# Pooling attention into a maxout feed-forward: the attention output of batches 3 to 7 turned by the DMA crossbar instead of TensorE

## The chip, the cores and the metric

The kernel runs on one core of a Trainium2 chip. The metric is the device time of one execution in microseconds, the median of several runs. The profile is one execution taken by the hardware profiler; its span is a little shorter than the timed run.

A core has five engines that work at the same time and meet at semaphores: TensorE (PE; PEld is its weight load), VectorE (DVE), ScalarE (ACT), GpSimd (POOL) and SyncE (SP), which here only issues DMAs. Each engine takes its instructions in the order of the program.

## The reference

Attention with pooled keys and values, for 8 batches of 8 heads, 576 queries, 64 elements a head. Then a feed-forward layer over all 4608 tokens, with three weights whose results are joined by a maximum.

```python
k_p = k.reshape(B, H, 72, 8, D).mean(axis=3)       # 576 keys pooled to 72
v_p = v.reshape(B, H, 72, 8, D).mean(axis=3)
attn = softmax(q @ k_p^T / sqrt(D)) @ v_p          # B, H, S, D
x = attn.transpose(0, 2, 1, 3).reshape(4608, 512)
h = maximum(x @ w1, x @ w2, x @ w3)                # 512 -> 768
out = h @ w_out                                    # 768 -> 512, float32
```

## The kernel before

The feed-forward layer is the larger part. It runs in nine blocks of 512 tokens (the loop over `n`), each in 22 slots. `hidden(n)` has 18 slots: for each of six column blocks of 128 and each of the three weights, four matmuls of 128x512 (L272) into a PSUM tile of the group "pw", and then ACT (L277) and DVE (L280, L283) take the maximum into `hT`. `project(n)` has 4 slots of six matmuls (L305); ACT copies the result (L310) and SP stores it in two DMAs of 128 KB (L314). `hidden` reads `xT`, the attention output with the channels on the partitions, for all 4608 tokens.

The attention of batch b is cut into steps, which are laid between the slots. `PLAN` gives, for each step in turn, the slot of iteration n after which it is issued, for batch n+1; `PLAN1` does so for n=1. Steps that the plan leaves over run in the first eight slots of the next iteration (`side`). The steps of a batch are:

- `queries(b)`: four `turn_q` steps (TensorE transposes of q, L159, copied by ACT at L161), one `turn_k` (the pooled keys transposed, copied by DVE at L171), and eight `scores` steps, one per head (matmuls L194, exponential on ACT L199).
- `outputs(b)`: five chunks of 128 tokens, `v0` to `v4` and `x0` to `x4`. `values` (step v) multiplies by the pooled values (L223), and DVE divides by the sum (L229, L231) into the tile `xn`, tokens on the partitions. `turn_x` (step x) transposes it: four 128x128 transposes on TensorE (L214) into the PSUM tile `pxt`, and a copy by ACT (L218) into `xT`. The last chunk starts at token 448 and keeps its upper 64 tokens.

`turn_q`, `turn_k` and `turn_x` share one PSUM buffer, the tag "tr". Batches 576 tokens long and blocks of 512 tokens shift against each other: block 3 needs batch 3 up to its token 320, block 4 batch 4 up to 256, block 5 batch 5 up to 192, block 6 batch 6 up to 128, block 7 batch 7 up to 64.

k and v of batches 2 to 7 are pooled on POOL by folding (`fold`, L127 and L130). POOL also issues the loads of k, v and q from batch 3 on (`load_k` L71, `load_v` L77, `load_q` L86), into two buffers each. In iteration n POOL folds k of batch n+2, issues the load of k of batch n+3, folds v, and issues the loads of v and q. The POOL DMAs run in one queue (q0 on the page), those from SP in another (q1).

Of the kernel before, what the change touches and what calls it, by code (L numbers as in the profile page):

```python
# [14 lines left out]
def kernel(  # L15
# [11 lines left out]
    nc = tc.nc  # L27
    dt = mybir.dt
    F32, BF16, F16 = dt.float32, dt.bfloat16, dt.float16

    B, H, S, D = q.shape
# [22 lines left out]
    sb3 = ctx.enter_context(tc.tile_pool(name="sb3", bufs=3))  # L54
# [3 lines left out]
    kts, vts, qbs, kps, qTs, ets = {}, {}, {}, {}, {}, {}  # L58
# [7 lines left out]
    def load_k(b, eng, dtype=F32, parts=1):  # L66
        kts[b] = ld.tile([96, 6, POOL, D], dtype, name="kt", tag="kt")
        src = k[b].rearrange("h s d -> (h s d)").rearrange(
            "(p i j d) -> p i j d", p=96, i=6, j=POOL)
        n = 6 // parts  # L70
        return [eng.dma_start(out=kts[b][:, i:i + n], in_=src[:, i:i + n])  # L71
                for i in range(0, 6, n)][-1]

    def load_v(b, eng, dtype=F32, cuts=(0, H)):
        vts[b] = ld.tile([Sp, H, POOL, D], dtype, name="vt", tag="vt")
        src = v[b].rearrange("h (sp j) d -> sp h j d", j=POOL)
        return [eng.dma_start(out=vts[b][:, h:g], in_=src[:, h:g])  # L77
                for h, g in zip(cuts, cuts[1:])][-1]

# [17 lines left out]

    load_q(0)
    load_k(0, nc.sync, parts=3)
    warm = const.tile([128, 512], BF16, name="warm", tag="warm")  # L100
    nc.vector.memset(warm, 1.0)
    ident = const.tile([128, 128], BF16, name="ident", tag="ident")
    make_identity(nc, ident)
    identh = const.tile([128, 128], F16, name="identh", tag="identh")
    make_identity(nc, identh)
    load_v(0, nc.gpsimd, F16, (0, 4, 6, 8))
    for i in range(3):
        load_w(slice(256 * i, 256 * i + 256))
    load_k(1, nc.gpsimd, F16)
    load_q(1)  # L110
    early = load_v(1, nc.gpsimd, F16)
    nc.gpsimd.dma_start(
        out=wo_sb, in_=moe_w_out.rearrange("(jc p) c -> p jc c", p=128))
    after((load_k(2, nc.sync), load_v(2, nc.sync)), early)
    load_q(2)

# [6 lines left out]
    xT = const.tile([128, KCH, TOK], F16, name="xT", tag="xT")  # L123
# [85 lines left out]
        exp(ets[b][:, h, :], psc[0:Sp, 0:S])  # L209

    def turn_x(b, c0, keep, xn, tag, evac=nc.scalar.copy):
        pxt = psp.tile([128, KCH, 128], F16, name="pxt", tag=tag[0], bufs=tag[1])
        for kc in range(KCH):
            nc.tensor.transpose(  # L214
                pxt[:, kc, :],
                xn[:, kc // 2, 2 * (kc % 2):2 * (kc % 2) + 2, :], identh)
        g0 = S * b + c0
        evac(out=xT[:, :, g0 + keep:g0 + 128], in_=pxt[:, :, keep:128])  # L218

    def values(b, c0):  # L220
        pav = psp.tile([128, 2, 512], F32, name="pav", tag="att", bufs=2)
        for h in range(H):
            nc.tensor.matmul(  # L223
                pav[:, h // 4, 65 * (h % 4):65 * (h % 4) + 65],
                ets[b][:, h, c0:c0 + 128], vp_all[:, b, h, :],
                start=True, stop=True)
        pv = pav[:, :, 0:260].rearrange("p g (h e) -> p g h e", e=65)
        rcp = sb3.tile([128, 2, 4], F32, name="rcp", tag="rcp")
        nc.vector.reciprocal(out=rcp, in_=pv[:, :, :, 64])  # L229
        xn = sb3.tile([128, 2, 4, D], F16, name="xn", tag="xn")  # L230
        nc.vector.tensor_tensor(  # L231
            out=xn, in0=pv[:, :, :, 0:D],
            in1=rcp.to_broadcast([128, 2, 4, D]), op=ALU.mult)
        return xn
# [5 lines left out]
    def queries(b):  # L240

        new_et(b)
        for m, (n0, n1) in enumerate(((0, 5), (5, 10), (10, 14), (14, 18))):
            turn_q(b, n0, n1, nc.scalar.copy, TR)
            yield
            if m == (3 if b == 2 else 2):
                turn_k(b)
                yield
        for h in range(H):
            scores(b, h)  # L250
            yield

    def outputs(b, order="v0 v1 x0 v2 x1 v3 x2 v4 x3 x4", tag=TR, evac=nc.scalar.copy):


        xns = {}
        for step in order.split():
            i = int(step[1])
            c0, keep = CHUNKS[i]
            if step[0] == "v":  # L260
                xns[i] = values(b, c0)
            else:
                turn_x(b, c0, keep, xns[i], tag, evac)
            yield
# [121 lines left out]
    pool_v(0, 6, 8, PW, nc.vector.tensor_copy)  # L386
    scores2(0)
    xn0 = [values(0, c0) for c0, _ in CHUNKS[:2]]
    heat(1)
    turn_x(0, 0, 0, xn0[0], PW)  # L390
    scores2(2)
    heat(1)
    turn_x(0, 128, 0, xn0[1], PW, nc.vector.tensor_copy)
    scores2(4)
    heat(1)
# [25 lines left out]
    for slot, _ in enumerate(hidden(0, hT0)):  # L421
# [4 lines left out]
        if slot > 24:  # L426
            h = 4 * (slot - 25)
# [14 lines left out]

    def batch(b):
        yield from queries(b)
        yield from outputs(b, *(("v0 v1 x0 v2 x1 x2 v3 x3 v4 x4",) if b == 2 else ()))


    PLAN = (2, 4, 5, 6, 8, 8, 9, 10, 11, 12, 13, 14, 15, 16, 17, 18, 18, 19, 19, 20,
            20, 21)
    PLAN1 = (9, 11, 13, 15, 19, 20, 21, 22, 23, 24, 25, 26, 26, 27, 28, 28, 29, 29, 30,  # L450
             30)
    for n in range(1, TOK // NB):
        if n + 2 < B:
            fold_k(n + 2, nc.gpsimd)
            if n + 3 < B:
                load_k(n + 3, nc.gpsimd)
            fold_v(n + 2)
            if n + 3 < B:
                load_v(n + 3, nc.gpsimd)
                load_q(n + 3)  # L460
        hT = new_hT()
        nxt = batch(n + 1) if n + 1 < B else iter(())
        plan = PLAN1 if n == 1 else PLAN
        slot = 0
        for part in (hidden(n, hT), project(n, hT)):
            for _ in part:
                if slot < 8:
                    next(side, None)
                for _ in range(plan.count(slot)):
                    next(nxt, None)  # L470
                slot += 1
        side = nxt
# [30 lines left out]
```

The softmax here doesn't subtract the row's maximum and nothing guards it: scores larger than these inputs give would overflow.

## Time and profile before

| what | value |
|---|---|
| time, median of 3 runs | 264.18 us (264.04 to 264.33) |
| span of the profile | 262.3 us, granted TensorE clock 0.995 |
| busy: PE, DVE, ACT, POOL | 95%, 51%, 48%, 45% |
| one iteration, n=2 to 5 (from first L305 to first L305) | 26.8 us |
| of it TensorE busy | 26.75 us |
| POOL's last fold ends | 161.5 us |

The page's busy shares are averages over the span. The chain that ended last is followed back from the last instruction, at each step to what released it; time on it is time that the end depends on. An iteration's times are best read there or in the timeline of one engine.

### The profile page before, as it was taken

What the parts mean: (1) busy time and instruction counts of PE and PEld (TensorE: products, weight loads), DVE (VectorE), ACT (ScalarE), POOL (GpSimd) and SP (SyncE); (2) the same over time, 40 slices, a digit from 0 to 9 for tenths busy, and PEclk for the clock granted to TensorE, in tenths of its full rate; (3) what the DMA queues carried; (4) which work ended last, traced back from release to release, by engine and by line L of the source; (5) the groups of instructions that cost most, each with busy time, mean ns of one, the idle gap of its engine ahead of it and who ended that gap; (6) DMA issues with size and microseconds to landing.
All of it is one profiled execution on the core that took longest, in us unless ns stands there. A gap on an engine that the chain in (4) does not pass through costs nothing.

```text
span 262.3 us, 4747 instructions
## 1 busy us (share of the span) xinstructions
PE 250.3 (95%) x1902; PEld 142.6 (54%) x1902; DVE 132.7 (51%) x243; ACT 125.9 (48%) x225; POOL 117.6 (45%) x84
## 2 busy tenths in 40 slices
PE   7899999988997999999999999999999999999992
PEld 3678556675554555555555555555555554444441
DVE  4567561766344546364635463556446554523430
ACT  1464237243754574548464746464656463132221
POOL 8653000999899999899790896000000000000000
PEclk9999999999999999999999999999999999999998
DMA  7999999886698975987987705100510042015006
GB/s 185 202 197 209 199 234 226 257 202 113 157 238 180 196 182 115 231 266 139 215 239 180 113 4 132 28 2 0 121 42 0 2 110 50 4 41 119 0 12 152
DMA packets 21027, 34.73 MB, mean 132 GB/s; under 512 B 2668, under 2 KB 13548, under 8 KB 20428
## 3 DMA queue, kind: packets, MB, share of 16 engines
q0 software_dynamic: 14048, 21.44, 42.0%
q1 hardware_dynamic: 6796, 12.85, 19.3%
q8 instruction: 15, 0.25, 0.4%
q10 hardware_dynamic: 160, 0.13, 0.2%
q14 instruction: 8, 0.07, 0.1%
HBM read 34.60 MB, written 9.44 MB: 168 GB/s over the span
## 4 chain that ended last, share of the span: by engine, by line
PE 87%; DVE 4%; ACT 4%; issue 1%; DMA 1%; SPq 0%; DVEq 0%
PE pw L272 49%; PE po L305 16%; PE psc L194 6%; PE pav L223 4%; PE pqt L159 3%; PE pxt L214 3%; PE wm L326 2%; ACT xT L218 2%; PE pvp L148 1%; DVE t L280 1%; DMA out_dram<-osb 1%; ACT et L199 1%; DVE xn L231 1%; PE pkt L166 1%; DVE kz L171 1%
## 5 line engine op out<-in xcount | busy, mean ns | idle before, releaser
L272 PE MATMUL pw<-xT,mw 128*128 128x512 f16 (+1 forms) x720 | 158.1, 358 | 0.9 <-ACT xT L218 0.7
L272 PEld LDWEIGHTS <-mw 128*128 128x128 f16 x720 | 64.3, 98 | 48.5 <-issue 0.8
L280 DVE TENSOR_TENSOR t<-t,pw 128x512 f16<-128x512 f16 (+1 forms) x60 | 38.0, 633 | 75.2 <-PE pw L272 46.3
L277 ACT CAST t<-pw 128x512 f16<-128x512 f32 (+1 forms) x60 | 32.6, 543 | 41.6 <-PE pw L272 39.0
L305 PE MATMUL po<-mwo,hT 128*128 128x512 f16 (+1 forms) x222 | 51.5, 373 | 0.0
L199 ACT ACTIVATE et<-psc 72x576 f16<-72x576 f32 (+2 forms) x62 | 40.4, 661 | 16.1 <-PE psc L194 16.1
L283 DVE TENSOR_TENSOR hT<-t,pw 128x512 f16<-128x512 f16 (+1 forms) x60 | 37.9, 632 | 11.0 <-PE pw L272 7.8
L127 POOL TENSOR_TENSOR vt<-vt 72x2048 f32<-72x2048 f32 (+1 forms) x12 | 41.2, 3432 | 4.5 <-DMA vt<-in_v_dram 4.0
L127 POOL TENSOR_TENSOR kt<-kt 96x1536 f32<-96x1536 f32 (+1 forms) x12 | 31.5, 2622 | 23.2 <-DMA kt<-in_k_dram 22.6
L310 ACT COPY osb<-po 128x512 f32<-128x512 f32 (+1 forms) x36 | 20.8, 579 | 38.7 <-PE po L305 38.5
L305 PEld LDWEIGHTS <-hT 128*128 128x128 f16 x222 | 19.9, 97 | 19.4 <-DVE hT L283 1.7
L231 DVE TENSOR_TENSOR xn<-pav,rcp 128x512 f16<-128x512 f32 x40 | 27.6, 691 | 1.4
L194 PE MATMUL psc<-qT,kz 128*128 128x64 bf16 (+3 forms) x192 | 25.6, 246 | 1.2 <-DVE kz L171 1.2
L161 ACT COPY qT<-pqt 128x512 bf16<-128x512 bf16 (+1 forms) x25 | 15.9, 637 | 21.5 <-PE pqt L159 21.5
L194 PEld LDWEIGHTS <-kz 128*128 128x128 bf16 x192 | 17.5, 98 | 15.0 <-DVE kz L171 2.0
L218 ACT COPY xT<-pxt 128x512 f16<-128x512 f16 (+1 forms) x34 | 18.6, 547 | 4.3 <-PE pxt L214 4.2
L223 PEld LDWEIGHTS <-et 72*128 72x128 f16 x320 | 15.2, 98 | 4.6 <-issue 0.5
L223 PE MATMUL pav<-vp,et 72*128 72x65 f16 x320 | 17.2, 194 | 0.4 <-ACT et L199 0.4
L214 PEld LDWEIGHTS <-xn 128*128 128x128 f16 x160 | 11.7, 97 | 10.7 <-DVE xn L231 3.1
L229 DVE RECIPROCAL rcp<-pav 128x8 f32<-128x8 f32 x40 | 8.2, 204 | 18.4 <-PE pav L223 18.3
L214 PE MATMUL pxt<-identh,xn 128*128 128x128 f16 x160 | 15.5, 219 | 2.0 <-DVE xT L218 0.7
L159 PEld LDWEIGHTS <-qb 128*128 128x128 bf16 x144 | 10.0, 97 | 7.9 <-issue 2.4
(43 smaller groups left out, 116.8 us busy)
## 6 DMA issues: line engine op xcount, KB each, us to landing
out_dram<-osb SPq DMA_DIRECT2D x70, 128.0 KB, 2.4
kt<-in_k_dram POOLq DMA_DIRECT2D x5, 1152.0 KB, 8.3
vt<-in_v_dram POOLq DMA_DIRECT2D x5, 1152.0 KB, 10.0
qb<-in_q_dram POOLq DMA_DIRECT2D x7, 576.0 KB, 13.3
mw<-in_moe_w_dram POOLq DMA_DIRECT2D x9, 256.0 KB, 10.0
kt<-in_k_dram SPq DMA_DIRECT2D x3, 384.0 KB, 4.8
kt<-in_k_dram SPq DMA_DIRECT2D x1, 1152.0 KB, 10.0
vt<-in_v_dram SPq DMA_DIRECT2D x1, 1152.0 KB
```

Of the source, the lines that this page charges most:

```text
L127: e.tensor_tensor(out=t[:, :, 0:n, :], in0=t[:, :, 0:n, :], in1=t[:, :, n:2 * n, :], op=ALU.add)
L194: nc.tensor.matmul(out, kz_all[b % 2][:, f % 2, h, :], qTs[b][:, n + i0:n + i1, 64 * (h % 2):64 * (h % 2) + 64], start=True, stop=True)
L199: nc.scalar.activation(out=out, in_=in_, func=FT.Exp, scale=1.0 / 64.0)
L214: nc.tensor.transpose(pxt[:, kc, :], xn[:, kc // 2, 2 * (kc % 2):2 * (kc % 2) + 2, :], identh)
L218: evac(out=xT[:, :, g0 + keep:g0 + 128], in_=pxt[:, :, keep:128])
L223: nc.tensor.matmul(pav[:, h // 4, 65 * (h % 4):65 * (h % 4) + 65], ets[b][:, h, c0:c0 + 128], vp_all[:, b, h, :], start=True, stop=True)
L231: nc.vector.tensor_tensor(out=xn, in0=pv[:, :, :, 0:D], in1=rcp.to_broadcast([128, 2, 4, D]), op=ALU.mult)
L272: nc.tensor.matmul(pw, w_sb[wi][:, kc, bass.ts(jc, 128)], xT[:, kc, col], start=(kc == 0), stop=(kc == KCH - 1))
L277: nc.scalar.copy(out=t, in_=pw)
L280: nc.vector.tensor_tensor(out=t1, in0=t, in1=pw, op=ALU.max)
L283: nc.vector.tensor_tensor(out=hT[:, jc, c0:c1], in0=t, in1=pw, op=ALU.max)
L305: nc.tensor.matmul(po, hT[:, jc, bass.ts(mm, 128)], wo_sb[:, jc, c], start=(jc == 0), stop=(jc == JCH - 1))
```

## The change

The chunks of batches 3 to 7 no longer go through TensorE, PSUM and ACT. SP issues a transposing DMA that reads `xn` in SBUF and writes `xT` in SBUF. This is to free TensorE of the transposes. The tile `xn` gets six buffers instead of three. The steps of each batch but batch 2 run in the order v0 x0 v1 x1 and so on, and the plan has one more entry, so that all steps of a batch are done within the iteration: the query transposes start at slot 0 instead of 2, and x0 follows v0 in slot 16.

The loads of k and v from batch 3 on are cut into pieces of 1 KB: a k load into runs of 256 elements (it had runs of all of a partition's 12 KB), a v load into two DMAs, one for each half of the eight rows that are pooled (runs of 2 KB before). The smaller pieces are to let other transfers in between.

```diff
 def load_k
-        return [eng.dma_start(out=kts[b][:, i:i + n], in_=src[:, i:i + n])
+        return [eng.dma_start(out=kts[b][:, i:i + n], in_=src[:, i:i + n],
+                              max_dma_last_dim=256 if b > 2 else None)
                 for i in range(0, 6, n)][-1]
 def load_v
         src = v[b].rearrange("h (sp j) d -> sp h j d", j=POOL)
+        if b > 2:
+            for j in (0, 4):
+                eng.dma_start(out=vts[b][:, :, j:j + 4], in_=src[:, :, j:j + 4])
+            return
 def turn_x
+        if b > 2:
+            g0 = S * b + c0
+            nc.sync.dma_start_transpose(
+                out=xT[:, :, g0 + keep:g0 + 128],
+                in_=xn.rearrange("p g h d -> p (g h d)")[keep:128])
+            return
 def values
-        xn = sb3.tile([128, 2, 4, D], F16, name="xn", tag="xn")
+        xn = sb3.tile([128, 2, 4, D], F16, name="xn", tag="xn", bufs=6)
 def batch
-        yield from outputs(b, *(("v0 v1 x0 v2 x1 x2 v3 x3 v4 x4",) if b == 2 else ()))
+        yield from outputs(b, "v0 v1 x0 v2 x1 x2 v3 x3 v4 x4" if b == 2
+                           else "v0 x0 v1 x1 v2 x2 v3 x3 v4 x4")
-    PLAN = (2, 4, 5, 6, 8, 8, 9, 10, 11, 12, 13, 14, 15, 16, 17, 18, 18, 19, 19, 20,
-            20, 21)
+    PLAN = (0, 2, 4, 5, 7, 8, 9, 10, 11, 12, 13, 14, 15, 16, 16, 17, 17, 18, 18, 19,
+            19, 20, 20)
```

## The prediction

> **What bounds the kernel now.** I read the page first: busy shares, the slices, the chain that ended last, the groups. Each row of the groups gives busy time, then the mean of one.
>
> ```profile
> PE 250.3 (95%) x1902; PEld 142.6 (54%) x1902; DVE 132.7 (51%) x243; ACT 125.9 (48%) x225; POOL 117.6 (45%) x84
> ...
> DMA  7999999886698975987987705100510042015006
> ...
> PE 87%; DVE 4%; ACT 4%; issue 1%; DMA 1%; SPq 0%; DVEq 0%
> ...
> L218 ACT COPY xT<-pxt 128x512 f16<-128x512 f16 (+1 forms) x34 | 18.6, 547 | 4.3 <-PE pxt L214 4.2
> ...
> L214 PE MATMUL pxt<-identh,xn 128*128 128x128 f16 x160 | 15.5, 219 | 2.0 <-DVE xT L218 0.7
> ```
>
> TensorE is the bound. ACT and DVE stand at half, and the DMA engines are near full only until about slice 22 (145 us). So a cut in TensorE's own instructions counts in full; ACT's copies count only where TensorE waits for them. The 219 ns of a transpose is a latency in the pipeline and not its price. The price is in the chain in order of time (start, length, what), here at the end of iteration n=3 and the start of n=4:
>
> ```profile
> 160.02 0.22 PE pxt L214 x4
> 160.25 0.26 PE pav L223 x8
> 160.51 1.31 PE po L305 x6
> 161.82 0.02 issue
> 161.84 0.25 ACT osb L310
> 162.09 0.23 issue
> 162.32 0.60 ACT xT L218
> 162.92 0.04 issue
> ```
>
> Four transposes of one chunk take 0.22 us, 55 ns each. The chain leaves TensorE at 161.82: in slot 0 of the next iteration the last chunk (x4) needs the one "tr" PSUM buffer, which ACT is still emptying from x3. Four L272 matmuls start at 161.86 and need 0.86 us, to 162.72; the transposes start at 162.96. TensorE loses 0.24 us.
>
> The third view is the timeline of one engine, for POOL (loads) and for the stores.
>
> ```profile
> 99.11 0.86 POOL L77 DMA_DIRECT2D vt<-in_v_dram  x1
> 99.96 0.78 POOL L86 DMA_DIRECT2D qb<-in_q_dram  x1
> ...
> 108.06 0.56 POOL L71 DMA_DIRECT2D kt<-in_k_dram  x1
> ```
>
> And the instructions of the tile osb in 103 to 110 us (end of n=2), then the store line L314 in 156 to 190 us (no loads left):
>
> ```profile
> L314 SPq DMA_DIRECT2D out_dram<-osb x8: 466/574/1353, 103.5 to 109.6; - x8
> DMA to landing us min/median/max: 7.0/7.4/10.6
> ...
> L314 SPq DMA_DIRECT2D out_dram<-osb x15: 466/467/827, 157.1 to 189.3; - x15
> DMA to landing us min/median/max: 2.2/2.3/4.1
> ```
>
> The same 128 KB store from SP lands in 2.3 us on quiet DMA engines, and in 7.4 us when a v load and a q load are in flight. The new transposes go down the same queue, move the same 128 KB, and TensorE will wait for some of them. This pair of numbers is the heart of the forecast.
>
> **What the Trainium skill says.** (1) "VectorE: DVE Perf Modes", The three transpose paths: a 128x128 bf16 transpose is 390 ns on TensorE and 1309 ns through the DMA crossbar. The trace has 55 ns of TensorE time in a stream, so the TensorE figure isn't what is saved here. No run yet shows a crossbar transpose. (2) "DMA: Bandwidth & Descriptors", Anatomy of one DMA: a fixed cost near 2 us for most DMAs; the quiet 2.3 us of the trace agrees. (3) Same page, Queues, rings and completion order: each DMA engine goes round the queues at packet granularity. The 7.4 us agrees with long waits for a turn. It is what smaller pieces of k and v can shorten.
>
> **The change part by part.** Let T be the start of the first L305 group of an iteration. Batches 3 to 7 are made in n=2 to 6.
>
> Removed from TensorE: 25 chunks x 4 = 100 transposes x 55 ns = 5.5 us, all on the path. Removed waits: 0.24 us at slot 0 of n=3 to 7, 1.2 us. Removed from ACT: 25 copies of xT; they were hidden behind TensorE apart from these waits, so nothing more. Sum: -6.7 us.
>
> Plan: values keep slots 16 to 20 and scores 8 to 15; query transposes move to slots 0, 2, 4, 7 and the keys from 6 to 5. In n=2 slots 0 to 2 still hold x3, v4, x4 of batch 2, on TensorE. So x3 and the first query transposes now meet in slot 0 on the one "tr" buffer. In the trace x3's transposes end at 81.02, ACT copies it from 81.31 to 81.90: +0.9 us. Slot 2 already had such a meeting (0.46 us wait at 84.44), so it adds nothing. In n=3 to 6 no transposes of xn are left there.
>
> Loads: v becomes two DMAs, k goes from 96 long runs to 1152 pieces. A POOL issue is 0.57 us for k and 0.86 us for v (576 runs); the difference over 480 runs is 0.6 ns a run. So k costs about +0.65 and v +0.87: 1.5 us of POOL a batch. It is hidden: the keys of batch 3 are folded at 71.1 and used in n=2 about slot 5, near 85; its values at 80.9, used near 100; batch 7's values at 161.5, used after 200. A batch takes POOL 18.3 us against TensorE's 26.8, so the margin grows. Slower DMA from smaller pieces is bounded likewise: 14 us of margin is over half of a batch's POOL time. Cost taken: 0. The extra xn buffers only keep DVE from waiting for the transposes to read.
>
> The new wait. Every transpose is a DMA on SP behind stores. SP's issue cost isn't in the trace for a transpose: below by a store, 0.47 us; above by the Trainium skill's column for earlier generations ("DMA: Bandwidth & Descriptors", under Why a DMA increments its semaphore): 631 cycles, and 32 cycles a tile. With tiles of 16x128 as its constraints table implies, 32 tiles give 1655 cycles, 1.4 us at SyncE's 1.2 GHz ("Trainium Kernel Development and Optimization", NeuronCore Architecture), an estimate. I take 1.0. Landing L from the start of issue: at least a quiet store plus a little, 2.5 us; at most 7.4 us as in the crowded window. I take the middle, 4.95, where loads are in flight, since smaller pieces should shorten the wait for a turn, but the q loads keep their size; where none are, 2.5.
>
> Which chunk does the next iteration need? hidden(n+1) starts at T + 4x1.30 + 3x0.26 = T+6.0 and reads tokens up to 512(n+2): in n=2 chunks 0 to 2 of batch 3, in n=3 and 4 chunks 0 and 1, in n=5 and 6 chunk 0. From the timeline of DVE in n=4 (T=181.99) xn of chunk 0 is ready at T+0.2, chunk 1 at T+1.6, chunk 2 at T+2.7 (its values come 0.2 sooner than now).
> - n=2: SP issues x1 from T+1.6 to 2.6, then the two stores of the first project step (0.47 to 0.6 us each) to T+3.7, then x2. It lands at T+3.7+4.95 = T+8.65: TensorE waits 2.7 us.
> - n=3: x1 lands at T+1.6+4.95 = T+6.6: 0.6 us.
> - n=4: the loads are nearly over, L=2.5: free. n=5, 6: T+0.2+L, free even at 5.8.
> Behind a waiting SP stand only later stores; five osb buffers cover them. TensorE in order holds everything behind the first L272, hence full price.
>
> Sum: 264.2 - 6.7 + 0.9 + 2.7 + 0.6 = 261.7 us.
>
> **Rivals.**
> Hidden transposes: L=2.5 throughout. Then n=2 waits 0.2 us, the others nothing: 264.2 - 6.7 + 0.9 + 0.2 = 258.6 us. For it: 128 KB is little beside 200 GB/s, and the pieces are cut for this. Against: the 7.0 us minimum in the very window where x0 to x2 are issued.
> Starved transposes, slower than before: L=7.4 where loads are crowded, n=2 to 4, POOL being later than now by some 1.5 us a batch. Waits T+3.7+7.4-6.0 = 5.1, then twice 1.6+7.4-6.0 = 3.0: 264.2 - 5.8 + 11.1 = 269.5 us. For it: the store rows. Against: in n=3 now stores land in 3.4 us (median).
> Serial crossbar, slower: four blocks of 1309 ns one after another, 5.2 us a chunk, SP or the crossbar the bound. n=2: 0.2+5.2x2+1.0+5.2 = T+16.8, waits 10.8; n=3 and 4: T+10.6, 4.6 each; n=5 and 6 T+5.4, free: 264.2 - 5.8 + 20 = 278.4 us. Against: the 1309 ns is likely to hold mostly fixed cost.
>
> **How the numbers follow.** Forecast case 0.45, hidden 0.22, starved 0.18, serial 0.07; 0.08 lies between forecast and starved, where the waits return all of the gain. Predicted is 261.7. The range goes from just under the hidden case, 258.0, to just over the starved one, 270.0; the serial case and half of the odd ones stay outside. Faster by over 0.2% (under 263.65): 0.67; within: 0.07; slower: 0.26.
>
> **What would show it.** TensorE should have 100 fewer L214 matmuls and ACT 25 fewer xT copies; an iteration from n=5 on should be 26.82 - 1.1 - 0.24 = 25.5 us from one first L305 to the next. The first L272 of n=3 should wait for a DMA into xT, 1 to 5 us, that of n=4 under 2 us, later ones not. SP's transposes should take 0.5 to 1.4 us to issue, and land in 4 to 6 us near 105 us and in 2.5 us after 160. POOL should finish the last fold 5 to 10 us later with nobody waiting. The forecast is wrong if transposes land slower than 6 us on quiet engines, if a transpose stops the stores or loads beside it, or if TensorE waits in n=5 or 6.

## The result, and the profile after

The changed kernel takes 276.15 us (274.14 to 276.67, four runs) against 264.25 us: ratio 1.043, 95% interval 1.038 to 1.049. It is slower by 4.3%.

The page of the changed kernel: busy shares, the granted clock in 40 slices, the packets, the chain by engine, and the first group (L283 is now the line of the first feed-forward matmul).

```profile
PE 246.6 (90%) x1801; PEld 137.5 (50%) x1802; DVE 132.1 (48%) x243; ACT 115.1 (42%) x200; POOL 128.0 (47%) x89
...
PEclk9999999999999999757999999999999999999998
...
DMA packets 34385, 37.66 MB, mean 137 GB/s; under 512 B 15068, under 2 KB 25948, under 8 KB 34268
...
q1 hardware_dynamic: 19116, 15.80, 27.1%
...
PE 75%; DMA 11%; DVE 8%; ACT 2%; issue 2%; POOL 1%; POOLq 0%; DVEq 0%
...
L283 PE MATMUL pw<-xT,mw 128*128 128x512 f16 (+1 forms) x720 | 159.6, 360 | 15.5 <-DMA xT<-xn 14.6
```

TensorE has some 100 instructions fewer, ACT 25, and both are less busy. The DMA engines, 1% of the chain before, are 11% of it. The 14.6 us at the end of the last row are waits of `hidden` for a transpose, two of them. The chain in order of time shows the large one, at the end of n=2 (start, length, what):

```profile
106.41 1.30 PE po L316 x6
107.71 0.28 PE pav L234 x8
108.17 14.41 DMA xT<-xn
122.62 1.89 PE pw L283 x4
124.51 0.53 PE pqt L164 x5
125.04 2.52 PE pw L283 x8
```

x2 of batch 3 was issued at 108.17 and landed 14.4 us later. TensorE had finished its last L316 matmul at 109.3 and stood still for 13.4 us. Then a second loss begins: four matmuls take 1.89 us instead of 0.86. The table of stretches (length, then busy time of PE, PEld, DVE, ACT, POOL, then clock, DMA share, GB/s) shows why:

```profile
122.60:124.60 2.00, 1.98 (x7) 0.88 (x8) 0.00 (x0) 0.06 (x1) 1.36 (x2) 0.50 1.44 198
124.60:126.60 2.00, 2.00 (x10) 0.91 (x8) 0.00 (x0) 1.17 (x2) 0.00 (x0) 0.52 1.13 153
126.60:128.60 2.00, 2.00 (x15) 1.06 (x14) 1.38 (x2) 0.69 (x1) 0.00 (x0) 1.00 1.43 225
```

The clock granted after the wait is half for 3.9 us. (It had fallen to half within the wait, near 112.8, some 3.5 us after TensorE stopped.) From 122.62 to 127.56 the chain has 4 matmuls in 1.89 us, 5 in 0.53 and 8 in 2.52, where a full clock takes 0.86, 0.28 and 1.73: 2.1 us lost.

The difference of the spans is 274.9 - 262.3 = 12.6 us. The parts: -5.5 (100 transposes) -1.2 (waits in slot 0) +0.9 (the meeting of x3 and the first query transposes) +1.2 (a new wait, below) +13.4 and +1.2 (x2 at n=2, x1 at n=3) +2.1 (clock) = +12.1. The rest of 0.5 us is not assigned.

The tile xT answers how the transposes behave: first those issued at 103 to 105 us (x0 and x1 of batch 3), then those of 197 us and later, when no load is left.

```profile
L219 SPq DMA_TRANSPOSE xT<-xn x2: 1313/1578/1842, 103.5 to 105.0; - x2
DMA to landing us min/median/max: 12.1/12.7/13.2
...
L219 SPq DMA_TRANSPOSE xT<-xn x10: 1188/1232/1422, 197.6 to 233.3; - x10
DMA to landing us min/median/max: 2.4/2.5/4.0
```

A transpose costs SP 1.2 us and lands in 2.5 us on quiet DMA engines, about as a store of the same 128 KB. Beside v5, q5 and k6 (the loads of batches 5 and 6) the same instruction takes 12 to 14 us to land, and the issue of x2 alone keeps SP for 4.2 us. How the two kinds meet can be read from the DMA queues in one stretch, 119 to 121.2 us (packets, MB, share):

```profile
q0 software_dynamic: 86, 0.35, 47.4%
q1 hardware_dynamic: 94, 0.04, 37.3%
```

In this stretch q0 (the loads) and q1 (transposes and stores) send about the same number of packets, but q0 moves nine times the bytes. It does not hold for the whole wait: from the issue of x2 to its landing q0 sends 808 packets with 1.61 MB, q1 1842 with 0.87 MB. Over the whole kernel q1 has 12,320 packets and 2.95 MB more than before (19,116 and 15.80 MB against 6796 and 12.85 MB). The 25 transposes move 20 x 131 KB + 5 x 66 KB = 2.95 MB, so their packets average 240 bytes: a chunk of 128 KB is over 500 packets, some 32 on each of 16 DMA engines. The Trainium skill says that the rounds between the queues go by packets ("DMA: Bandwidth & Descriptors", Queues, rings and completion order). The stretch of 119 to 121.2 us agrees with it, and this stream has very small packets.

### The profile page after: what moved, and what is told of

Its sections match the earlier page's. It is cut to its first block, busy times and chain, and to the rows that moved or that the text cites. A ratio compares the mean times of both kernels' runs of the same rounds, so it can differ in the third digit from the quotient of the medians.

```text
span 274.9 us, 4608 instructions
## 1 busy us (share of the span) xinstructions
PE 246.6 (90%) x1801; PEld 137.5 (50%) x1802; DVE 132.1 (48%) x243; ACT 115.1 (42%) x200; POOL 128.0 (47%) x89
## 3 DMA queue, kind: packets, MB, share of 16 engines
q1 hardware_dynamic: 19116, 15.80, 27.1%
## 4 chain that ended last, share of the span: by engine, by line
PE 75%; DMA 11%; DVE 8%; ACT 2%; issue 2%; POOL 1%; POOLq 0%; DVEq 0%
PE pw L283 45%; PE po L316 15%; DMA xT<-xn 8%; PE psc L199 5%; PE pqt L164 3%; DVE kz L176 3%; DMA vt<-in_v_dram 3%; PE pav L234 3%; DVE hT L294 1%; PE pvp L153 1%; DVE t L291 1%; PE pxt L225 1%; DVE xn L242 1%; ACT xT L229 1%; ACT et L204 1%
## 5 line engine op out<-in xcount | busy, mean ns | idle before, releaser
L283 PE MATMUL pw<-xT,mw 128*128 128x512 f16 (+1 forms) x720 | 159.6, 360 | 15.5 <-DMA xT<-xn 14.6
L283 PEld LDWEIGHTS <-mw 128*128 128x128 f16 x720 | 64.7, 98 | 66.0 <-DMA xT<-xn 15.6
L316 PE MATMUL po<-mwo,hT 128*128 128x512 f16 (+1 forms) x222 | 51.5, 373 | 0.0
L294 DVE TENSOR_TENSOR hT<-t,pw 128x512 f16<-128x512 f16 (+1 forms) x60 | 38.0, 633 | 13.3 <-PE pw L283 10.7
L316 PEld LDWEIGHTS <-hT 128*128 128x128 f16 x222 | 19.9, 97 | 19.4 <-DVE hT L294 1.7
L234 PEld LDWEIGHTS <-et 72*128 72x128 f16 x320 | 15.9, 98 | 7.5 <-issue 0.5
L91 POOL DMA_DIRECT2D qb<-in_q_dram x9 | 7.0, 783 | 19.3 <-PE pqt L164 16.9
L164 PE MATMUL pqt<-ident,qb 128*128 128x128 bf16 x144 | 13.3, 222 | 2.7 <-ACT xT L229 1.4
L135 POOL TENSOR_TENSOR kp<-kt 96x384 bf16<-96x384 f32 x12 | 11.7, 991 | 0.5
```

Source lines behind the costliest of these rows:

```text
L164: nc.tensor.transpose(pqt[:, n - n0, :], qf[:, 128 * n:128 * n + 128], ident)
L234: nc.tensor.matmul(pav[:, h // 4, 65 * (h % 4):65 * (h % 4) + 65], ets[b][:, h, c0:c0 + 128], vp_all[:, b, h, :], start=True, stop=True)
L283: nc.tensor.matmul(pw, w_sb[wi][:, kc, bass.ts(jc, 128)], xT[:, kc, col], start=(kc == 0), stop=(kc == KCH - 1))
L294: nc.vector.tensor_tensor(out=hT[:, jc, c0:c1], in0=t, in1=pw, op=ALU.max)
L316: nc.tensor.matmul(po, hT[:, jc, bass.ts(mm, 128)], wo_sb[:, jc, c], start=(jc == 0), stop=(jc == JCH - 1))
```

## The experiments

Theories: P, the transposes wait for the packets of the loads in flight. F, they are slow by themselves, in one queue behind stores or in the crossbar. S, the 1 KB pieces do the harm.

**1. The pieces alone.** The kernel before with the edits of `load_k` and `load_v` only.

> The kernel before with the loads of k and v of batches 3 to 7 in pieces of 1 KB and nothing else. Theory P (a transposed chunk is 512 small packets, 32 on each DMA engine, and each waits for a turn behind a packet of the loads; the pieces are no part of the loss): 264 us, within 0.3% of before, POOL some 7 us more busy, its last fold later with nobody waiting. Rival S (the small pieces themselves clog the DMA engines): slower than before by 2 us or more, stores in 103 to 112 us landing later than 7.4 us.

Measured: 264.14 us against 264.02, ratio 1.0006 (0.9994 to 1.0018). POOL is busy 128.2 us instead of 117.6, and nobody waits for it. The eight stores of 103.7 to 109.5 us land in 8.8 to 9.6 us (7.0 to 10.6 before), with no effect on the time. The pieces alone are free; S falls as a cause. On POOL's queue a piece is not a packet: in the packet records of the traces a v load is 288 packets of 4096 bytes with the pieces and without them, and a k load goes from 96 packets of 12,288 bytes to 288 of 4096.

This run also has the loads and the stores of the changed kernel without its transposes. What the DMA engines carry over 104 to 122 us, here and then in the changed kernel:

```profile
DMA packets 1889, 4.02 MB, mean 223 GB/s; under 512 B 288, under 2 KB 800, under 8 KB 1888
...
DMA packets 2904, 3.09 MB, mean 172 GB/s; under 512 B 1800, under 2 KB 2312, under 8 KB 2903
```

The stores issued from 106 to 108 us, here (L319) and then in the changed kernel (L325):

```profile
L319 SPq DMA_DIRECT2D out_dram<-osb x3: 467/606/731, 106.0 to 107.8; - x3
DMA to landing us min/median/max: 9.0/9.3/9.5
...
L325 SPq DMA_DIRECT2D out_dram<-osb x2: 546/566/586, 106.9 to 107.5; - x2
DMA to landing us min/median/max: 14.2/14.4/14.7
```

The load k6, issued at 112.3 us in both, lands in 9.8 us here and in 15.5 us beside the transposes. So transposes and loads together move less than stores and loads do, though packets are in flight on the engines for more of the time (a DMA share of 1.17 against 0.90 over 104 to 122 us), and the stores and the loads come late as well. The prediction had named this as a sign of being wrong. Why the engines move less was not tried.

**2. The transposes with whole loads.**

```diff
 def load_k
-                              max_dma_last_dim=256 if b > 2 else None)
+        return [eng.dma_start(out=kts[b][:, i:i + n], in_=src[:, i:i + n])
...
 def load_v
-        if b > 2:
-            for j in (0, 4):
-                eng.dma_start(out=vts[b][:, :, j:j + 4], in_=src[:, :, j:j + 4])
-            return
```

> The changed kernel with the loads of k and v as before (runs of 12 KB and 2 KB). Theory P: the v load runs as packets of 4096 bytes either way, so the wait of the first matmul of n=3 for x2 stays at 10 to 15 us; the 12 KB packets of k make a turn longer where a k load is in flight; 276 to 282 us. Rival S: the wait falls below 6 us and the time below 268 us.

Measured: 285.58 us, with runs from 274 to 290, so no ratio is given. The chain of the profiled run (287.49 us), at the same place:

```profile
106.19 1.10 PE po L311 x6
107.29 26.76 DMA xT<-xn
```

In this run x2 took 26.8 us instead of 14.4. But the fastest of the four took 274.17 us, less than the changed kernel's 276.15, so it is not shown that the pieces shorten the wait. Shown is that the loss stays without them: no run is near the 268 us of rival S. The theory's 10 to 15 us was wrong for the profiled run: v6, issued at 117.25, came into the same stretch, and over 112 to 120 us the engines moved only some 100 GB/s.

**3. Loads of v and q held until x2 has landed.** In n=2 to 4, `turned` holds the transposes of `turn_x`.

```diff
-            if n + 3 < B:
+            if n == 1:
                 load_v(n + 3, nc.gpsimd)
                 load_q(n + 3)
...
+        if n > 1 and n + 3 < B:
+            after(load_v(n + 3, nc.gpsimd) + load_q(n + 3), turned[n + 1, 256])
```

> The changed kernel with the loads of v and q of batches 5, 6 and 7 held back until x2 of the same iteration has landed, so that no load is in flight beside the transposes that TensorE waits for. Theory P: each of x0 to x2 lands within 2.3 to 3 us of its issue, the wait of 13.4 us at the start of n=3 falls below 0.5 us, TensorE keeps its full clock there, and the time is 259 to 261 us, faster than the kernel before. Rival F (the transposes are slow by themselves, one after another behind the stores on the queue of SP): x2 still lands after 8 us or more and the time stays above 270 us.

Measured: 261.25 us, ratio 0.989 (0.986 to 0.992). The profiled run is the longest of the five (263.93 us; the others took 260.56 to 261.63). With the same queue, the same stores ahead and the same crossbar, x2 lands in 3.7 us:

```profile
106.60 1.10 PE po L316 x6
107.71 3.71 DMA xT<-xn
```

TensorE waits 2.0 us instead of 13.4, not under 0.5 as expected: SP issues x2 4.2 us after the first L316 group, and it needs 3.7 us where 1.8 were left. So the time also ends a little above the 259 to 261 us expected. Half clock follows this wait too (0.50 from 112.7 to 116.0 us); the four other runs have a mean granted clock of 0.999 or 1.00, so there it can hardly have fallen. F falls as the main cause; what is left of it is those 2 us.

**4. Batch 3 on TensorE, batches 4 to 7 through the crossbar.** The order of batch 3's steps and the plan of n=2 are those of the kernel before.

```diff
-        if b > 2:
+        if b > 3:
```

> The changed kernel with batch 3 left on TensorE (its order and the plan of n=2 as before); batches 4 to 7 go through the crossbar. Its x4 runs in slot 0 of n=3 and meets the first query transposes there, about 0.9 us. Theory P: the 13.4 us wait is gone with its loss of clock (2 us); n=3 has v6 and q6 in flight and TensorE waits there for x1, 2 to 8 us, as chunk 1 needs 64 turns on each engine; n=4 to 6 run in 25.7 us; 262 to 268 us. Rival F: waits of 8 us or more at n=4 as well, above 270 us.

Measured: 262.01 us, ratio 0.992 (0.990 to 0.995), at the lower edge. At n=3 x1 lands 5.6 us after its issue and TensorE waits 1.44 us, less than the 2 to 8 us expected. From the timeline of TensorE (start, length, instruction, and in brackets the idle time before it):

```profile
136.33 1.02 PE L283 MATMUL pw<-xT,mw 128*128 128x512 f16 x4 [1.44 <-DMA xT<-xn]
```

The clock stays at 1.00 after it. So the transposes of batch 3 carried the loss.

**5. x2 the first transpose in the queue.** x0 and x1 of batch 3 on TensorE, x2 to x4 through the crossbar; batch 3 in the order v0 v1 x0 v2 x2 v3 x1 v4 x3 x4, with nearly the plan of before for n=2.

```diff
-        if b > 2:
+        if b > 3 or b == 3 and c0 > 128:
```

> The changed kernel with x0 and x1 of batch 3 on TensorE again and the steps of n=2 in the plan of before, so that x2 is the first transpose on the queue of SP beside v5 and q5; x3 and x4 of batch 3 and all of batches 4 to 7 go through the crossbar. Theory P: x2 has 32 turns of 0.2 to 0.28 us on each engine instead of 96 and lands 6 to 9 us after its issue; the first matmul of n=3 waits 4 to 7 us instead of 13.4. Rival L (a transpose gets through only when the loads are done, however few its packets): the wait stays at 11 us or more. Rival F (its own queue and the crossbar make it late): it lands within 4 us. Time by theory P 265 to 269 us.

Measured: 270.91 us, ratio 1.021 (1.018 to 1.024). x2 lands 11.5 us after its issue and TensorE waits 8.3 us. All three expectations missed. With two thirds of the packets taken away x2 lands only 2.9 us sooner after its issue; as it was also issued earlier, the wait is 5 us shorter. The split is not clean: x2 is issued 2.1 us after the v load here, 5.7 us after it in the changed kernel, so it has more of v5 beside it. Still, x2 needs 11.5 us here with no transpose ahead of it, and 3.7 us in run 3 with two ahead of it. Its own queue is a part of the delay, and the loads in flight are the larger part.

**6. v as fp16.** The load is one DMA again.

```diff
+        dtype = F16 if b > 2 else dtype
         vts[b] = ld.tile([Sp, H, POOL, D], dtype, name="vt", tag="vt")
-        if b > 2:
-            for j in (0, 4):
-                eng.dma_start(out=vts[b][:, :, j:j + 4], in_=src[:, :, j:j + 4])
-            return
```

> The changed kernel with v of batches 3 to 7 loaded as fp16 by the DMA and summed in fp16 on POOL; the load is whole again, and its packets are a quarter of a v packet's bytes (1 KB). Theory P: a turn behind v takes near 0.1 us, as behind q, instead of 0.2 to 0.28; the wait for x2 falls from 13.4 to 4 to 9 us and the time to 265 to 271 us. Rival B (the queues share by bytes or by time and not by turns): the wait stays at 11 us or more.

Measured: 268.14 us, ratio 1.013 (1.011 to 1.016). x2 lands in 6.0 us; TensorE waits 4.6 us there, within theory P's range. The load has a quarter of the bytes in a packet, but also half the bytes in all, and POOL issued it some 4 us earlier. The next runs try to take these apart.

**7 and 8. One load in flight.** As run 3, but only q is held (v5 in flight), or only v (q5 in flight). The edit of run 7 against run 3 is shown; in run 8 `load_v` and `load_q` change places.

```diff
-            if n == 1:
+            if n + 3 < B:
                 load_v(n + 3, nc.gpsimd)
+            if n == 1:
                 load_q(n + 3)
...
-            after(load_v(n + 3, nc.gpsimd) + load_q(n + 3), turned[n + 1, 256])
+            after(load_q(n + 3), turned[n + 1, 256])
```

> The version with held loads, but only the q loads of batches 5 to 7 are held; v5 is issued at 102 us and is the one load in flight beside the transposes of n=2 (packets of 4096 bytes, 18 on each DMA engine). Refined theory P: the transposes can lose at most the time of the load's own packets, 18 turns of 0.25 us, and a slow start of some 2 us; x2 lands 6 to 10 us after its issue (14.4 with v5, q5 and k6, 3.7 with none); TensorE waits 4 to 8 us at n=3. Rival Q (it is the q load with its 32 packets an engine that starves them): x2 lands within 5 us.

> The version with held loads, but only the v loads of batches 5 to 7 are held; q5 is the one load in flight beside the transposes of n=2 (packets of 1152 bytes, 32 on each engine, 0.106 us each). Refined theory P: 32 turns of 0.106 us, so x2 lands 4 to 7 us after its issue and TensorE waits 1.5 to 5 us at n=3. Rival Q: x2 lands 9 us or more after its issue, later than with v5 in flight.

The chain with v5 in flight, then with q5:

```profile
106.07 1.30 PE po L316 x6
107.48 8.50 DMA xT<-xn
```

```profile
105.92 1.18 PE po L316 x6
107.10 5.74 DMA xT<-xn
```

8.5 us with v5 (1.18 MB), 5.7 with q5 (0.59 MB), as the refined theory had it; rival Q falls. The times, 276.04 and 268.64 us, also hold waits at later iterations: with the hold, POOL's next v load falls just ahead of the transposes of n=3 (issued at 134.7, first L316 at 138.7), so these two say nothing on the best place for a load.

**9 and 10. The same bytes in packets of 1 KB.** v5 is issued by ACT on its own hardware queue, two DMAs of 1 KB pieces, q held; in slot 16 (run 9, shown), then in slot 18 (run 10).

```diff
+                if slot == 16 and 1 < n and n + 3 < B:
+                    load_v(n + 3, nc.scalar)
```

> As the run with v5 alone in flight, but v of batches 5 to 7 is issued by ACT in slot 16 on ACT's hardware queue, where a packet is one piece of 1 KB: the same bytes beside the same transposes, in packets of a quarter. Theory P (turns by packet): x0 to x2 get a turn every 0.06 to 0.1 us, x2 lands within 5 us of its issue and TensorE waits under 3 us at n=3. Rival B (what counts is the bytes of the load in flight): x2 lands as late as in that run, 6 to 10 us, as the bytes are the same.

> As the run with v in packets of 1 KB on ACT's queue, but issued in slot 18, near 105 us, so that v5 is in flight later than in the run with packets of 4096 bytes (issued at 102.8) and meets x2 in full. Theory P (turns by packet): x2 lands 6 us or less after its issue. Rival B (bytes in flight): 8.5 us or more, as with the large packets.

Measured: x2 lands in 6.0 us when v5 is issued at 101.0 us (270.95 us in all, ratio 1.026, 1.020 to 1.033), and in 8.2 us when it is issued at 104.7 us (284.24 us, two runs). The first misses theory P's 5 us and is no verdict, as the load started 1.8 us sooner than in run 7. The second lies between the two expectations and near the 8.5 us of run 7, but its load started 1.9 us later than there. On a straight line between the two, a load issued at 102.8 us as in run 7 would give some 7 us (an estimate). So packets of a quarter may be worth some 1.5 us, and the time at which the load comes is worth at least as much; neither theory is shown, and small packets alone don't save the transposes.

What the DMA queues carried from the issue of x2 to its landing, with the total size of the loads that were issued before it landed:

| case | loads, total size | of them moved in that time | transposes and stores moved | x2 lands in |
|---|---|---|---|---|
| run 3 | none | none | 0.45 MB | 3.7 us |
| run 8 | q5, 0.59 MB | 0.14 MB | 0.94 MB | 5.7 us |
| run 9 | v5, 1.18 MB, packets of 1 KB | 0.23 MB | 0.89 MB | 6.0 us |
| run 10 | the same, issued later | 0.91 MB | 0.78 MB | 8.2 us |
| run 7 | v5, 1.18 MB | 0.64 MB | 0.87 MB | 8.5 us |
| run 5 | v5, q5, k6, 2.95 MB | 1.69 MB | 0.87 MB | 11.5 us |
| changed | v5, q5, k6, 2.95 MB | 1.61 MB | 0.87 MB | 14.4 us |

More loads in flight mean a later landing, but the delay is not the bytes of the loads over one rate: over run 3 it is 2.0 us with 0.14 MB moved, 4.8 with 0.64 and 10.7 with 1.61. Two more things are in it. The loads also hold up the transposes ahead: from the issue of x0 to that of x2, q1 sends 79 packets in the changed kernel and 1096 in run 3, where x0 and x1 (512 each) are through by then. And the engines move less when transposes are among the loads (run 1). These runs don't tell how much each adds.

**11. The version put together.** x3 and x4 of batch 3, which nothing needs before n=4, and batches 4 to 7 through the crossbar; v and q of batches 6 and 7 held until x2 of the iteration; whole loads; the fourth query transposes in slot 8. For n=2 the plan is that of before with x4 added.

```diff
-        if b > 2:
+        if b > 3 or b == 3 and c0 > 256:
-    PLAN = (0, 2, 4, 5, 7, 8,
+    PLAN = (0, 2, 4, 5, 8, 8,
...
+        if n > 2 and n + 3 < B:
+            after([load_v(n + 3, nc.gpsimd)] + load_q(n + 3), turned[n + 1, 256])
```

> A version put together from the findings: through the crossbar go x3 and x4 of batch 3, which nothing waits for until 20 us later, and all chunks of batches 4 to 7; the loads of v and q of batches 6 and 7 are held until x2 of the iteration has landed; k and v in whole loads as before; the plan of n=2 as before, and from n=3 the fourth query transposes in slot 8 instead of 7. Theory P: 22 chunks x 0.22 us and five waits of 0.24 us less than before and no wait for a DMA anywhere: 258.0 us. Rivals F and L: TensorE waits for a transpose at n=3 or later, 261 us or more.

Measured: 257.42 us against 264.34, ratio 0.974 (0.972 to 0.976). The chain at the end of n=3, where the kernel before had its transposes and the wait in slot 0:

```profile
130.80 1.30 PE po L312 x6
132.10 0.26 PE pav L230 x8
132.36 1.30 PE po L312 x6
133.65 0.86 PE pw L279 x4
134.52 0.28 PE pqt L160 x5
```

TensorE goes from one iteration into the next without a gap, and it waits for no transpose anywhere.

**12. The same without the hold.**

```diff
-            if n < 3 and n + 3 < B:
+            if n + 3 < B:
-            after([load_v(n + 3, nc.gpsimd)] + load_q(n + 3), turned[n + 1, 256])
```

> The version put together, without the hold: v and q of batches 6 and 7 are loaded as soon as POOL comes to them. If the hold is what keeps TensorE from waiting, n=3 meets v6, q6 and k7 with 12 KB packets: a wait of 5 to 25 us there, the clock falling with it, 263 to 285 us. If the choice of chunks alone was enough: 257 to 258 us.

Measured: 261.90 us, ratio 0.991 (0.987 to 0.994): a wait of 2.8 us at n=3 and half clock behind it, less than the 5 us expected and 4.5 us in all. The timeline of TensorE:

```profile
136.43 1.89 PE L279 MATMUL pw<-xT,mw 128*128 128x512 f16 x4 [2.76 <-DMA xT<-xn]
```

So the hold is worth 4.5 us here, nearly as much as the 22 chunks that TensorE gave up (4.8 us).

## Why the prediction was wrong

- **What TensorE gains** was right. An iteration from the first L316 at 197.33 to that at 223.06 takes 25.73 us, 25.5 were forecast. The 0.24 us too much are one new wait in each of the five iterations, from the plan edit that was costed at nothing: with the keys in slot 5 and the last query transposes in slot 7, the copies of the keys still hold the "tr" buffer.

```profile
185.74 0.40 PE L164 MATMUL pqt<-ident,qb 128*128 128x128 bf16 x4 [0.23 <-DVE kz L176]
```

- **The meeting in slot 0 of n=2**, 0.9 us: right.
- **The pieces at no cost**: right (run 1). A k load costs POOL 1.84 us to issue, not 0.57 + 0.65 = 1.22, and in the changed kernel POOL's last fold ends 15.6 us later, not 5 to 10; nobody waited for either.
- **The quiet transpose**: right. 1.2 us of SP (1.0 taken) and 2.5 us to land (2.5 taken) where no loads are left, nothing lost in n=4 to 6. The rival of a serial crossbar, 5.2 us a chunk, falls.
- **The step that failed: "Landing L", taken as 4.95 where loads are in flight, with 7.4 as its upper end.** At n=3 it was near (5.5 us for x1, a wait of 1.24 us where 0.6 was forecast). At n=2 x2 needed 14.4 us, 9.5 more than taken, and it was issued 4.9 us after T instead of 3.7, as the issue of x1 kept SP for 1.8 us instead of 1.0 and the stores came later. The two make the wait 13.4 us instead of 2.7. L had been read from stores, a kind of DMA with few and large packets, and half of their excess was taken off for the pieces. The step from a store to a transpose did not hold: with the same loads in pieces stores land in 9.0 to 9.5 us (run 1), and with the transposes among them the transposes need 12.1 to 14.4 us and the stores 14.2 to 14.7, while the engines move 172 GB/s instead of 223. L was also counted from each transpose's own issue, as if x0 and x1 were no longer ahead of x2. That the loads in flight are the cause is shown by runs 3, 7 and 8 (3.7 us with none, 8.5 with v5, 5.7 with q5); how the engines share their time between the two stays open. The starved rival had the right cause and side, 269.5 us, and the same wrong kind of size, 7.4.
- **A term that the prediction put at nothing:** half clock after the wait, 2.1 us. The Trainium skill has it ("TensorE: Matmul & The Clock Gate", Part 1: The HAM clock gate): an idle TensorE falls to half rate after some 3.4 us. The runs agree that it is half, and the 3.5 us within the large wait agree with the time. But half clock also came after shorter waits, of 2.00 us (run 3), 2.38 us (run 9) and 2.76 us (run 12), and not after others of 2.10 us (run 9), 1.93 us (run 8), 1.44 or 1.24. So the length of the wait alone does not decide.

What stays open: why the engines move less when transposes and loads meet, and why x2 took 26.8 us in the profiled run with whole loads. From its issue to its landing the queues moved 2.59 MB of loads and 1.04 MB of transposes and stores there, 137 GB/s. Packets of 12 KB that hold up the crossbar's small ones on all engines together would fit the 100 GB/s seen over 112 to 120 us; that wasn't tried by itself. Nor was it settled why the gain of the version put together (6.9 us) is 0.9 us over the sum.

## What to carry to other kernels

A transfer that takes the place of an instruction on the bounding engine has to be priced at its landing time beside the loads of that very stretch, with what stands ahead of it in its own queue, and compared with the time until the first consumer. Another kind of transfer is a poor measure of it: here stores landed in 7.0 to 10.6 us where the transposes took 12.1 to 14.4. Measure one in place before building on it. Give the crossbar only those chunks that nothing needs soon, and hold prefetches with slack until the urgent ones have landed; here that turned a loss of 4.3% into a gain of 2.6%. And a single wait on TensorE can cost more than its length: after the 13.4 us here the clock stayed at half for another 3.9 us, 2.1 us lost.

## What the runs showed of the hardware that was not expected

- A 128x512 fp16 transpose in the crossbar is as quick as a store of its size (2.5 us against 2.3 us to land, on quiet engines), but goes out as over 500 packets of about 240 bytes.
- Transposes and loads together slow each other and the stores: 172 GB/s over 104 to 122 us, against 223 in run 1, which has the same loads and stores and no transposes.
- The engines can all but stop with much outstanding. In 102 to 124 us of the changed kernel, in slices of 0.55 us, the rate falls to 28 and 10 GB/s near 112 us, in the first of them with the engines counted as busy, while x0 to x2, two stores, v5 and q5 were still on their way; the two lines are busy tenths and GB/s. Why was not tried:

```profile
DMA  0001757989999749999099999988995579579995
GB/s 0 0 0 38 98 134 231 298 216 231 173 189 180 145 144 195 189 145 28 10 116 115 123 202 205 162 109 118 356 351 182 182 150 212 182 142 298 342 228 167
```

- TensorE's half clock followed a wait for a DMA of 2.00 us and not one of 2.10. After waits of 4.6 us and more it lasted from 3.4 us (run 10) to 5.8 us (run 6).
